# A spectral mixer with an MLP on one core: second batch's sums moved to GpSimd, its first stage ahead of the MLP, the last quarter of w_in converted between transform and MLP

## The chip, the core and the metric

The kernel runs on one NeuronCore of a Trainium2 chip. Its engines work side by side, each in the order of its own queue: PE (TensorE: matmuls, weight loads shown as PEld), DVE (VectorE), ACT (ScalarE, which also issues DMAs), POOL (GpSimd) and SP (SyncE, which here only issues DMAs). The metric is the time of one execution on the device in microseconds (us); lower is better.

## The reference, cut to what matters

```python
X = np.fft.rfft(x, axis=1)                    # x: 8 batches, 3008 positions, 256 columns
Yr = Xr @ w_r - Xi @ w_i + b_r
Yi = Xr @ w_i + Xi @ w_r + b_i
Y  = soft_threshold(Yr, 0.01) + 1j * soft_threshold(Yi, 0.01)
y  = np.fft.irfft(Y, n=3008, axis=1)
h  = y.reshape(24064, 256) @ w_in             # 256 x 2048
out = np.maximum(0.01 * h, h) @ w_out         # 2048 x 256
```

The MLP's two weights arrive as float64, and are turned into float32 (or a high and a low float32 part) on the chip.

## The kernel before, in words

The 3008-point transform is split as 47 x 64. For one batch the forward side is: `fwd`, the first stage over the 47, on seven tiles `xin` of 512 columns (the last has 256), which needs the sum and the difference of each tile's two halves and writes its results to `u_dram`; then `mid`, which for each of 12 pairs of rows reads `u`, does the second stage (`stage_b`: tile `ef`), multiplies by the spectral weights (`proj`: `kc`, then the threshold `t`, then `zf`), and turns back (`stage_g`: `v`, written to `v_dram`). The inverse's last stage (`inverse`: tiles `vin`, `odd`, `y`) makes the MLP's input `yc`, of which `forms` makes seven forms, each as a high and a low part (`yh`, `yl`), because the first MLP product is done with seven block products in place of eight. The MLP runs over 47 chunks of 512 tokens, in 8 steps each. One step (`moe_a`, `moe_b`, `moe_o`) has 21 matmuls with w_in, 12 with w_out, and on DVE five operations that end in `gl`.

Batches 0 and 1 are loaded ahead. Batch 0 goes through `fwd` and `mid` alone, before any MLP work; the later batches' forward sides are woven into the MLP as fill. The stretch between the last pair of batch 0's `mid` and the first MLP steps is called the turn here. In it also run the inverse of the first chunk and `fwd` of batch 1 (`stage_a1`), which before the change has no sums: for each of its two results it multiplies both halves of a tile, with the constants `fa0`, `fa1`, and a negated copy of `fa1` for the difference (`fa{h}` and `fa{2h}`), and so takes four products a tile. Five of its seven tiles are written ahead of the MLP in program order (`fp.to(0.69)`), two in the MLP's first steps.

The weights' conversions stand beside this: `convert_win` turns one of four quarters of w_in (`win_raw` into `win_hi`, `win_lo`, through the tiles `cva`, `cvq`, `ws`), the first two ahead of `mid` of batch 0, the others at its sixteenths 3 and 8, and `load_wout` turns one of eight pieces of w_out at each `next(wout)` (seven DVE operations and three of ACT), two in the turn and then one in each MLP step.

A scheduler reorders each engine's queue by its own estimates, within what `tc.issue_after` allows; so the order on an engine isn't the order of the code. Tiles with the same tag share buffers: a new tile waits until the old one's last reader is through. `forms` of the first chunk writes a `yh` buffer that held `ws`, and of the second one that held an `xin` of batch 1.

Of the kernel before, what the change touches and what calls it, by code (L numbers as in the profile page):

```python
# [8 lines left out]
F32 = mybir.dt.float32  # L9
# [11 lines left out]
P = 128  # L21
PA = NK1 * NG
# [8 lines left out]
def spectral_mlp_kernel(  # L31
# [18 lines left out]
    D = w_r.shape[0]  # L50
    DF = w_in.shape[1]
    NF = DF // P
    NH = D // P
# [10 lines left out]
    sb = ctx.enter_context(tc.tile_pool(name="sb", bufs=2))  # L64
# [4 lines left out]
    def bank(tag, bufs):  # L69
        return ps.tile([P, 512], F32, name=tag, tag=tag, bufs=bufs)  # L70

    def products(dst, pairs):

        terms = []
        for l, r in pairs:
            terms += [(l[0], r[0]), (l[0], r[1]), (l[1], r[0])] if len(l) == 2 else [(l[0], r[0])]
        for i, (a, b) in enumerate(terms):
            last = nc.tensor.matmul(dst, a, b, start=(i == 0), stop=(i == len(terms) - 1))  # L78
        return last
# [46 lines left out]
    def float64_parts(raw, a, q):  # L126


        wl, wh = raw[:, :, 0], raw[:, :, 1]
        u = a.bitcast(U32)  # L130
        act.mul(q, wl, 2.0 ** -52)
        act.activation(a, wh.bitcast(F32), AF.Abs, scale=2.0 ** 16)
        dve.tensor_scalar(a, a, F64_MIN * 2.0 ** 16, F64_MAX * 2.0 ** 16, ALU.max, ALU.min)
        dve.tensor_scalar(u, u, 4, 1, ALU.logical_shift_left, ALU.logical_shift_right)
        dve.scalar_tensor_tensor(u, wh, 0x80000000, u, ALU.bitwise_and, ALU.bitwise_or)
        dve.tensor_scalar(wl, u, 0xFF800000, None, ALU.bitwise_and)
        dve.tensor_mul(q, q, wl.bitcast(F32))
# [19 lines left out]
    def convert_win(c):  # L157


        a, q, s = win_tmp  # L160
        float64_parts(win_raw[c], a, q)
        dve.tensor_add(a, a, q)
        a = a.rearrange("p (j q i m) -> p j q i m", j=NH, q=2, i=2)
        a11, a12, a21, a22 = (a[:, j, :, i] for i in range(2) for j in range(2))
        dve.tensor_add(s[:, 0], a21, a22)
        dve.tensor_sub(s[:, 2], a11, a21)
        dve.tensor_sub(s[:, 1], s[:, 0], a11)
        dve.tensor_sub(s[:, 3], a12, s[:, 1])
        hi, lo = (w[:, :, 2 * c:2 * c + 2] for w in consts["win"])
        for k, w in ((slice(0, 2), a[:, :, :, 0]), (2, a22), (slice(3, 7), s)):  # L170
            act.copy(hi[:, k], w)
            last = dve.tensor_sub(lo[:, k], w, hi[:, k].bitcast(F32))
        return last
# [42 lines left out]
    def fwd(b):  # L216
        ud = dram.tile([2, NK1, NG * NS, D], F32, name="u_dram", tag="u_dram", bufs=NPRE + 1)
        u_dram[b] = ud
        uv = ud.rearrange("c k (g s) d -> c (k g) (s d)", g=NG)
        x_t, s_t = {}, {}  # L220

        def load(c):
            cols = slice(2 * c * D, min(2 * c + 2, NS) * D)
            n = cols.stop - cols.start
            if b < NPRE:
                tag, bufs = (XT, XT1)[b][c]
                x2 = sb.tile([PA, 2, 2 * D], F32, name="xin", tag=tag, bufs=bufs)
                x_t[c] = [x2[:, h, :n] for h in range(2)]
            else:
                x_t[c] = [  # L230
                    sb.tile([PA, 2 * D], F32, name=f"xin{h}", tag="uv"[h], bufs=3 - h)[:, :n] for h in range(2)
                ]
            for h, t in enumerate(x_t[c]):
                if b == 0:
                    (act if h else sync).dma_start(t, x[b, h, :, cols])
                else:
                    with tc.issue_after(reads[-1].ins):
                        sync.dma_start(t, x[b, h, :, cols])

        def fold(c):  # L240
            xa, xb = x_t[c]
            n = xa.shape[1]
            eng = pool if b else dve
            xs = sb.tile([PA, 2 * D], F32, name="xs", tag="e", bufs=1)[:, :n] if b else xs3[:, c % 3, :n]
            eng.tensor_add(xs, xa, xb)
            eng.tensor_sub(xa, xa, xb)
            s_t[c] = [(xs,), (xa,)] if b < NPRE else [xs, xa]

        def split(c, h):
            t = s_t[c][h]  # L250
            n = t.shape[1]
            z = sb.tile([PA, 2, 2 * D], F32R, name="xz", tag="z", bufs=1)
            xh, xl = z[:, 0, :n], z[:, 1, :n]
            dve.tensor_copy(xh, t)
            dve.tensor_sub(xl, t, xh.bitcast(F32))
            s_t[c][h] = (xh, xl)

        def stage_a(c, h):
            t = x_t[c][h]
            n = t.shape[1]  # L260
            pa = (bank("psf", 2) if b else bank("psh", 4))[:PA, :n]
            products(pa, [(consts[f"fa{h}"] if b else consts[f"fa{h}32"], s_t[c][h])])
            t = x_t[c][1 - h]
            cp = act.copy(t, pa)
            if b == 0:
                turned[:] = [cp]
            st = (act if b else sync).dma_start(uv[h, :, 2 * c * D:2 * c * D + n], t)
            if b == 0:
                written.append(st)

        def stage_a1(c):

            n = x_t[c][0].shape[1]
            pas = [(bank("psf", 2) if c in (4, 5) else bank("psh", 4))[:PA, :n] for _ in range(2)]
            for h in range(2):
                with tc.issue_after(turning[NPAIR - 2].ins):
                    products(pas[h], [
                        (consts[f"fa{h}32"], (x_t[c][0],)), (consts[f"fa{2 * h}32"], (x_t[c][1],))])
            for h in range(2):
                act.copy(x_t[c][h], pas[h])  # L280
                sync.dma_start(uv[h, :, 2 * c * D:2 * c * D + n], x_t[c][h])

        if b == 1:
            for c in range(NX):
                load(c)
                yield 0
            for c in (0, 1, 2, 3, 6, 4, 5):
                stage_a1(c)
                yield 6 * x_t[c][0].shape[1]
            return  # L290

        ahead = 2 if b >= NPRE else NX
        for c in range(ahead):
            load(c)
        yield 4 * CS if b >= NPRE else 0
        fold(0)
        if b >= NPRE:
            split(0, 0)
        yield 0
        for c in range(NX):  # L300
            for h in range(2):
                if h == 0 and c + ahead < NX:
                    load(c + ahead)
                if h == 0 and c + 1 < NX:
                    fold(c + 1)
                stage_a(c, h)
                if b >= NPRE and (c + h < NX):
                    split(c + h, 1 - h)
                yield 3 * x_t[c][h].shape[1]
# [335 lines left out]
    FWD = NS * 6 * D  # L645


    fa32 = sb.tile([PA, 3, PA], F32, name="fa32", tag="xi", bufs=1)
    for h in range(2):
        sync.dma_start(fa32[:, h], fa[h])  # L650
    for h in range(3):
        consts[f"fa{h}32"] = (fa32[:, h],)
    xs3 = sb.tile([PA, 3, 2 * D], F32, name="xs3", tag="yl")
    f0 = Stream(fwd(0), FWD)
# [22 lines left out]
    act.copy(bz[:1], brow[:1])  # L677
    act.copy(bz[32:33], brow[32:33])
    dve.tensor_sub(bz[32:33], brow[32:33], bz[32:33].bitcast(F32))
    act.mul(fa32[:, 2], fa32[:, 1], -1.0)  # L680
    convert_win(0)
    with tc.issue_after(turned[0].ins):
        split_consts()
# [12 lines left out]
    wout = load_wout()  # L696
    for i in range(1, 17):
        m0.to(i / 16)
        if i in (3, 8):
            convert_win(2 + i // 8)  # L700
        if 5 <= i < 12:
            next(fp.gen)
        if i == 13:
            next(wout)
    m0.finish()
    fp.to(0.69)
    for p in due[0]:
        v_load(p)
    for eh in range(NH):
# [1 line left out]
            inverse(p, eh)  # L711
    for _ in forms(0):
        pass
    next(wout)
    next(wout)


# [2 lines left out]
    for i, pos in enumerate(moe()):  # L720
        if i % 2 == 0 and len(converted) < NQ:
            with tc.issue_after(made[0].ins):
                next(wout, None)
        if i in (2, 4):
            with tc.issue_after(parted[0].ins), tc.issue_after(parted[1].ins):
                next(fp.gen)
        while cur + 1 < NB - 1 and pos >= (read[cur + 1] if cur >= 0 else 0):
            for s in streams:
                s.finish()
            cur += 1  # L730
            streams = ([Stream(fwd(cur + 1), FWD + 4 * CS)] if cur else []) + [mids[cur]]
        frac = (pos - read[cur]) / (read[cur + 1] - read[cur]) if cur + 1 < NB else 1
        if cur == 0:
            frac = max(0, frac - 0.2) * 1.25
        work = frac / 0.95 * sum(s.total for s in streams)
        with tc.issue_after(converted[-1].ins) if cur == 0 else nullcontext():
            for s in streams:
                s.to(work / s.total)
                work = max(0, work - s.total)
# [103 lines left out]
```

## Time and profile before

| | |
|---|---|
| median of 3 runs | 2600.41 us (2598.28 to 2602.9) |
| profiled execution | 2600.34 us, span 2598.6 us |
| mean granted PE clock | 0.993 |
| busy share of the span | PE 98%, DVE 73%, ACT 64%, POOL 9% |
| DMA, mean | 64 GB/s |

All times in the rows are counted from the start of the span. A row of the timeline has its start, its length, engine, line, operation, the tile written and the tiles read, and in brackets the idle time before it and what ended that. A matmul in float32 shows as two rows or passes in the trace (x4 is two such matmuls), and one instruction in the orders below. The lengths of matmuls overlap: what one takes of PE is read from start to start.

### The profile page before, as it was taken

What the parts mean: (1) busy time and instruction counts of PE and PEld (TensorE: products, weight loads), DVE (VectorE), ACT (ScalarE), POOL (GpSimd) and SP (SyncE); (2) the same over time, 40 slices, a digit from 0 to 9 for tenths busy, and PEclk for the clock granted to TensorE, in tenths of its full rate; (3) what the DMA queues carried; (4) which work ended last, traced back from release to release, by engine and by line L of the source; (5) the groups of instructions that cost most, each with busy time, mean ns of one, the idle gap of its engine ahead of it and who ended that gap; (6) DMA issues with size and microseconds to landing.
All of it is one profiled execution on the core that took longest, in us unless ns stands there. A gap on an engine that the chain in (4) does not pass through costs nothing.

```text
span 2598.6 us, 42643 instructions
## 1 busy us (share of the span) xinstructions
PE 2537.5 (98%) x16300; PEld 2281.5 (88%) x16300; DVE 1897.1 (73%) x3403; ACT 1668.5 (64%) x3174; POOL 229.6 (9%) x180
## 2 busy tenths in 40 slices
PE   5999999999999999999999999999999999999999
PEld 4689888999889998899988999889998889999998
DVE  7687786776777778777786777877777777767675
ACT  5766665776556666567665666566666667655564
POOL 0001121100110001100021000210002000000000
PEclk8999999999999999999999999999999999999999
DMA  8621132111221113211132111321113221101000
GB/s 259 179 85 50 48 89 72 54 47 48 82 78 49 45 41 90 75 55 51 33 97 68 49 49 37 104 67 49 49 36 101 64 58 48 44 17 32 9 17 17
DMA packets 119912, 165.13 MB, mean 64 GB/s; under 512 B 13601, under 2 KB 69917, under 8 KB 119709
## 3 DMA queue, kind: packets, MB, share of 16 engines
q1 hardware_dynamic: 79120, 115.55, 14.6%
q10 hardware_dynamic: 40589, 46.87, 7.1%
q8 instruction: 128, 2.10, 0.4%
q14 instruction: 75, 0.61, 0.1%
HBM read 86.60 MB, written 75.76 MB: 62 GB/s over the span
## 4 chain that ended last, share of the span: by engine, by line
PE 89%; DVE 3%; DMA 2%; ACT 1%; issue 0%; ACTq 0%; SPq 0%; DVEq 0%
PE pso L576 38%; PE psh L92 34%; PE psf L78 11%; PE psf L480 3%; PE psf L343 3%; DMA u<-u_dram 1%; DMA u_dram<-xin 1%; DVE yl L506 0%; DVE gl L563 0%; DMA raw<-w_out_dram 0%; DVE gf L557 0%; ACT gh L561 0%; DVE yt L511 0%; ACT gf L559 0%; DVE yc L512 0%
## 5 line engine op out<-in xcount | busy, mean ns | idle before, releaser
L92 PE MATMUL psh<-yh,win_hi 128*128 128x256 f32 x2632 | 752.3, 286 | 13.8 <-DVE gf L546 10.6
L92 PE MATMUL psh<-yl,win_hi 128*128 128x256 f32 x2632 | 738.3, 280 | 0.6 <-DVE yl L506 0.5
L92 PE MATMUL psh<-yh,win_lo 128*128 128x256 f32 x2632 | 737.9, 280 | 0.0
L576 PE MATMUL pso<-gh,wout_hi 128*128 128x512 f32 x1504 | 593.9, 395 | 0.0
L576 PE MATMUL pso<-gl,wout_hi 128*128 128x512 f32 x1504 | 591.1, 393 | 0.5 <-DVE gl L563 0.5
L576 PE MATMUL pso<-gh,wout_lo 128*128 128x512 f32 x1504 | 590.4, 393 | 0.0
L563 DVE TENSOR_TENSOR gl<-gf,gh 128x1024 fp32r<-128x1024 f32 x376 | 471.8, 1255 | 92.7 <-ACT gh L561 90.6
L92 PEld LDWEIGHTS psh<-yh,win_hi 128*128 128x128 f32 x2632 | 497.0, 189 | 30.7 <-DVE gf L546 15.4
L92 PEld LDWEIGHTS psh<-yl,win_hi 128*128 128x128 f32 x2632 | 497.0, 189 | 12.5 <-DVE yl L506 1.0
L92 PEld LDWEIGHTS psh<-yh,win_lo 128*128 128x128 f32 x2632 | 496.6, 189 | 0.2
L557 DVE TENSOR_TENSOR gf<-psh,u 128x512 f32<-128x512 f32 x376 | 259.1, 689 | 256.3 <-PE psh L92 255.1
L561 ACT CAST gh<-gf 128x1024 fp32r<-128x1024 f32 x376 | 396.4, 1054 | 7.1
L559 ACT ACTIVATE gf<-gf 128x768 f32<-128x768 f32 x376 | 320.0, 851 | 49.5 <-DVE gf L557 47.7
L576 PEld LDWEIGHTS pso<-gl,wout_hi 128*128 128x128 f32 x1504 | 282.5, 188 | 62.9 <-DVE gl L563 1.0
L576 PEld LDWEIGHTS pso<-gh,wout_hi 128*128 128x128 f32 x1504 | 283.1, 188 | 46.9 <-ACT gh L561 0.4
L576 PEld LDWEIGHTS pso<-gh,wout_lo 128*128 128x128 f32 x1504 | 282.9, 188 | 44.9
L556 ACT ACTIVATE gf<-psh 128x256 f32<-128x256 f32 x376 | 145.5, 387 | 266.6 <-PE psh L92 246.9
L542 ACT COPY p<-psh 128x256 f32<-128x256 f32 x376 | 140.1, 373 | 220.2 <-PE psh L92 219.1
L379 POOL TENSOR_TENSOR kb<-bias,kc 128x512 f32<-128x512 f32 x84 | 119.0, 1417 | 1530.6 <-ACT kc L376 1409.6
L543 DVE TENSOR_TENSOR u<-psh,p 128x256 f32<-128x256 f32 x376 | 158.6, 422 | 105.8 <-ACT p L542 103.5
L545 DVE TENSOR_TENSOR gf<-psh,u 128x256 f32<-128x256 f32 x376 | 159.3, 424 | 29.7 <-PE psh L92 2.0
L546 DVE TENSOR_TENSOR gf<-psh,gf 128x256 f32<-128x256 f32 x376 | 159.1, 423 | 9.0
(134 smaller groups left out, 3253.2 us busy)
## 6 DMA issues: line engine op xcount, KB each, us to landing
u<-u_dram SPq DMA_DIRECT2D x192, 128.0 KB, 2.7
v_dram<-v ACTq DMA_DIRECT2D x192, 128.0 KB, 2.4
out_dram<-ob SPq DMA_DIRECT2D x94, 256.0 KB, 2.1
vin<-v_dram SPq DMA_DIRECT2D x96, 240.0 KB, 3.5
xin<-x_dram SPq DMA_DIRECT2D x90, 240.0 KB, 3.0
u_dram<-xin ACTq DMA_DIRECT2D x72, 240.0 KB, 2.4
u_dram<-xin SPq DMA_DIRECT2D x24, 240.0 KB, 3.9
raw<-w_out_dram SPq DMA_DIRECT2D x8, 512.0 KB, 5.0
```

The costliest lines, as they stand in the source:

```text
L78: last = nc.tensor.matmul(dst, a, b, start=(i == 0), stop=(i == len(terms) - 1))
L92: mlp[:] = [nc.tensor.matmul(dst, a, b, start=start and i == 0, stop=i == 2, skip_group_check=True)]
L542: act.copy(p1, b1[:, lo])
L543: dve.tensor_add(u2, b1[:, hi], p1)
L545: dve.tensor_add(g[:, 3], b2[:, hi], u2)
L546: dve.tensor_add(g[:, 3], b2[:, lo], g[:, 3])
L556: act.activation(g[:, 0], b1[:, lo], AF.Prelu, alpha=SLOPE)
L557: dve.tensor_add(g[:, 1:3], b2.rearrange("p (k n) -> p k n", k=2), u2.unsqueeze(1).broadcast_to([P, 2, HT]))
L559: act.activation(g[:, 1:4], g[:, 1:4], AF.Prelu, alpha=SLOPE)
L561: cp = act.copy(gh, g)
L563: parted[:] = [cp, dve.tensor_sub(gl, g, gh.bitcast(F32))]
L576: mlp[:] = [nc.tensor.matmul(po, a[:, f, s], r[:, i], start=(f == 0 and j == 0), stop=(f == NF - 1 and j == 2),)]
```

## The change

Three things are done. GpSimd takes the sum and the difference of each of batch 1's seven tiles (`fold1`, 14 operations), writing the sum into the free half of the tile before it (a third slot in tile 4 serves the first); `stage_a1` then has two products a tile instead of four, the negated `fa1` goes, and the results of tiles 4 and 5 go to the `pso` banks instead of `psf`. All seven tiles of `stage_a1` stand ahead of the MLP (`fp.finish()`), none in its steps. The last quarter of w_in is converted behind `mid` instead of at its middle, in a tile of its own for `cva`; the third moves from sixteenth 3 to 4; and one piece of w_out instead of two is converted ahead of the MLP.

```diff
 def convert_win(c):
         a, q, s = win_tmp
+        if c == 3:
+            a = sb.tile([P, NH * NIN], F32, name="cva", tag="e", bufs=1)
...
 def load(c):   # in fwd
-                x2 = sb.tile([PA, 2, 2 * D], F32, name="xin", tag=tag, bufs=bufs)
+                spare = b == 1 and c == 4
+                x2 = sb.tile([PA, 3 if spare else 2, 2 * D], F32, name="xin", tag=tag, bufs=bufs)
                 x_t[c] = [x2[:, h, :n] for h in range(2)]
+                if b == 1:
+                    s_t[c] = x2[:, 1]
+                if spare:
+                    s_t[-1] = x2[:, 2]
...
+        def fold1(c):
+            xa, xb = x_t[c]
+            n = xa.shape[1]
+            xs = s_t[-1][:, :n]
+            s_t[-1] = s_t.pop(c)
+            pool.tensor_add(xs, xa, xb)
+            pool.tensor_sub(xa, xa, xb)
+            x_t[c] = [xs, xa]
+
         def stage_a1(c):
-            pas = [(bank("psf", 2) if c in (4, 5) else bank("psh", 4))[:PA, :n] for _ in range(2)]
+            pas = [(bank("pso", 2) if c in (4, 5) else bank("psh", 4))[:PA, :n] for _ in range(2)]
             for h in range(2):
                 with tc.issue_after(turning[NPAIR - 2].ins):
-                    products(pas[h], [
-                        (consts[f"fa{h}32"], (x_t[c][0],)), (consts[f"fa{2 * h}32"], (x_t[c][1],))])
+                    products(pas[h], [(consts[f"fa{h}32"], (x_t[c][h],))])
...
             for c in range(NX):
                 load(c)
                 yield 0
+            for c in (0, 1, 2, 3, 6, 4, 5):
+                fold1(c)
...
-    act.mul(fa32[:, 2], fa32[:, 1], -1.0)
...
-        if i in (3, 8):
-            convert_win(2 + i // 8)
+        if i == 4:
+            convert_win(2)
...
     m0.finish()
-    fp.to(0.69)
+    convert_win(3)
+    fp.finish()
...
     next(wout)
-    next(wout)
...
-        if i in (2, 4):
-            with tc.issue_after(parted[0].ins), tc.issue_after(parted[1].ins):
-                next(fp.gen)
```

What the scheduler makes of it: every engine's order is the same again from some 650 rows of PE on, where both have done the same work. The lines after the change are numbered 14 to 18 higher behind the first edits (L78 and L132 stay). On ACT, the last `ef` copy of batch 0 (its two sums open the last projection), before:

```order
L418 COPY v<-psh 128x512
L347 COPY ef<-psh 128x2x256
L420 DMA v_dram<-v 64x2x256
L396 COPY zf<-t 64x256
L400 ACTIVATE zf<-t,sign 64x256
```

and now, with the four zf instructions of pair 9 and a pair of stores ahead of it:

```order
L436 COPY v<-psh 128x512
L438 DMA v_dram<-v 64x2x256 x2
L414 COPY zf<-t 64x256
L418 ACTIVATE zf<-t,sign 64x256
L414 COPY zf<-t 64x256
L418 ACTIVATE zf<-t,sign 64x256
L365 COPY ef<-psh 128x2x256
```

The `ef` copy has moved behind pair 9's zf. Still on ACT, from the last pair's `kc` to the end of the transform (the last zf copies are pair 11's, the third `v` its result), before:

```order
L376 COPY kc<-pso 128x256
L318 DMA v_dram<-zero 48x256
L418 COPY v<-psh 128x512
L420 DMA v_dram<-v 64x2x256 x2
L418 COPY v<-psh 128x512
L396 COPY zf<-t 64x256 x2
L420 DMA v_dram<-v 64x2x256 x2
L418 COPY v<-psh 128x512
L132 ACTIVATE cva<-raw 128x512
```

and now:

```order
L394 COPY kc<-pso 128x256
L132 ACTIVATE cva<-win_raw 128x1024
L438 DMA v_dram<-v 64x2x256 x2
L436 COPY v<-psh 128x512
L336 DMA v_dram<-zero 48x256
L296 COPY xin<-pso 120x512
L438 DMA v_dram<-v 64x2x256 x2
L414 COPY zf<-t 64x256 x2
L296 COPY xin<-pso 120x512 x2
L436 COPY v<-psh 128x512
```

An activation of the quarter of w_in and a copy of the first stage stand ahead of the last zf, two more copies ahead of the last `v`. On PE, the turn from the last three `zf` products on (`fa` is the first stage of batch 1, `ga` the inverse), before:

```order
L78 MATMUL psh<-zf,w_105 128x512 x3
L78 MATMUL psh<-xin,fa_66 120x512 x8
L480 MATMUL psf<-ga,vin 128x128 x2
L78 MATMUL psh<-xin,fa_66 120x512 x2
L480 MATMUL psf<-ga,vin 128x128 x2
```

and now, from pair 10's on:

```order
L78 MATMUL psh<-zf,w_105 128x512
L78 MATMUL pso<-xin,fa_66 120x512 x3
L78 MATMUL psh<-zf,w_105 128x512
L78 MATMUL psh<-xin,fa_66 120x512 x3
L78 MATMUL pso<-xin,fa_66 120x512
L78 MATMUL psh<-xin,fa_66 120x512 x4
L498 MATMUL psf<-ga,vin 128x128 x2
L78 MATMUL psh<-xin,fa_66 120x512
L78 MATMUL psh<-xin,fa_66 120x256 x2
L498 MATMUL psf<-ga,vin 128x128 x10
```

Three products of the first stage now stand ahead of the last pair's, eight between it and the inverse, and three of 14 among the inverse's, where before it was none, eight and twelve of 20 (with the fences' next rows). On DVE, the third MLP step's end (`gl`) in the new order, with one whole piece of w_out (`cva`, `raw`, `cvq`, `wout_lo`) between two `gl`:

```order
L133 TENSOR_SCALAR cva<-cva 128x512
L134 TENSOR_SCALAR cva<-cva 128x512
L135 SCALAR_TENSOR_TENSOR cva<-raw,cva 128x512
L575 TENSOR_TENSOR gf<-psh,u_1051 128x512
L136 TENSOR_SCALAR raw<-cva 128x512
L137 TENSOR_TENSOR cvq<-cvq,raw 128x512
L203 TENSOR_TENSOR cva<-cva,wout_hi 128x512
L561 TENSOR_TENSOR u_1129<-psh,p_1128 128x256
L204 TENSOR_TENSOR wout_lo<-cva,cvq 128x512
L563 TENSOR_TENSOR gf<-psh,u_1129 128x256
L581 TENSOR_TENSOR gl<-gf,gh 128x1024
```

Before, six such pieces stood among the MLP's steps; now there are seven, and the second chunk's forms come ahead of the first `gl` instead of between the second and the fourth. SP's queue has stores of batch 1's first stage among its first four `vin` loads (three ahead of the first, three ahead of the second and third, two ahead of the fourth), where before they stood behind all four.

More of the change, by code (lines that the diff above doesn't have):

```diff
@@ L645, in spectral_mlp_kernel @@
     FWD = NS * 6 * D
-    fa32 = sb.tile([PA, 3, PA], F32, name="fa32", tag="xi", bufs=1)
+    fa32 = sb.tile([PA, 2, PA], F32, name="fa32", tag="xi", bufs=1)
     for h in range(2):
         sync.dma_start(fa32[:, h], fa[h])
-    for h in range(3):
+    for h in range(2):
         consts[f"fa{h}32"] = (fa32[:, h],)
```

## The prediction

> **What bounds the kernel now.** I read the page first (busy shares, chain), then the stretches around the hand-over from the first batch's transform to the MLP.
>
> ```profile
> PE 2537.5 (98%) x16300; PEld 2281.5 (88%) x16300; DVE 1897.1 (73%) x3403; ACT 1668.5 (64%) x3174; POOL 229.6 (9%) x180
> ...
> PE 89%; DVE 3%; DMA 2%; ACT 1%; issue 0%; ACTq 0%; SPq 0%; DVEq 0%
> ...
> 60.00:80.00 20.00, 18.91 (x97) 14.98 (x97) 18.09 (x34) 18.33 (x38) 0.00 (x0) 1.00 0.82 247
> 80.00:100.00 20.00, 19.01 (x94) 14.85 (x93) 11.64 (x23) 17.57 (x38) 0.30 (x1) 1.00 0.36 94
> 100.00:120.00 20.00, 17.40 (x48) 8.02 (x47) 10.44 (x19) 9.61 (x18) 0.00 (x0) 0.91 0.67 191
> 120.00:140.00 20.00, 17.27 (x92) 13.01 (x91) 16.24 (x37) 14.30 (x33) 0.00 (x0) 0.95 0.51 150
> 140.00:160.00 20.00, 18.28 (x99) 14.59 (x98) 18.17 (x37) 13.21 (x26) 0.00 (x0) 0.96 0.49 147
> 160.00:180.00 20.00, 19.39 (x124) 17.40 (x124) 19.86 (x39) 13.61 (x24) 0.00 (x0) 1.00 0.17 47
> 180.00:200.00 20.00, 20.00 (x136) 18.42 (x135) 13.06 (x23) 13.22 (x25) 2.58 (x2) 1.00 0.17 54
> ```
>
> The columns of a stretch are its length, busy us of PE, PEld, DVE, ACT and POOL, the granted clock, the DMA share and GB/s. PE is the bound, full from 180 us on. The order of every engine is the same again some 70 us later, so the change is worth what it does to the moment at which PE is through with the same MLP work near 180 us. Two stages lie before that: the turn (about 97 to 130 us), where PE idles little because the second batch's first stage fills it, and the ramp (130 to 180 us), where DVE, at 18.17 and 19.86 of 20 us, sets the pace while it converts w_out beside the MLP.
>
> ```profile
> 94.69 1.03 PE L78 MATMUL psf<-w,ef 128*128 128x256 f32 x4
> 97.52 1.02 PE L78 MATMUL psh<-zf,w 128*128 128x512 f32 x2
> 99.53 1.13 PE L78 MATMUL psh<-zf,w 128*128 128x512 f32 x2 [0.99 <-ACT zf L400]
> 103.26 1.48 PE L78 MATMUL psh<-zf,w 128*128 128x512 f32 x2 [2.60 <-ACT zf L396]
> 113.23 1.88 PE L78 MATMUL psh<-xin,fa 120*120 120x512 f32 x4
> 114.95 0.61 PE L480 MATMUL psf<-ga,vin 120*128 120x128 f32 x4
> 172.58 0.39 PE L576 MATMUL pso<-gl,wout_hi 128*128 128x512 f32 x1
> 172.81 0.39 PE L576 MATMUL pso<-gh,wout_hi 128*128 128x512 f32 x1
> 179.08 0.28 PE L78 MATMUL psf<-wr_hi,eh 128*128 128x256 f32 x1
> ```
>
> Here the last pair's projection begins at 94.69, the last three turns zf (pairs 9, 10, 11) stand at 97.52, 99.53 and 103.26, the last two after waits on ACT. The row at 179.08, the second batch's first projection, is my common point: in both orders exactly 162 products of w_in and 72 of w_out stand ahead of it.
>
> **The change, part by part.**
>
> *Half of the first stage's products go.* Two products of 512 columns take 114.95 - 113.23 = 1.72 us, 0.86 each. Twelve of 512 and two of 256 columns (half, 0.43) fall away: 11.2 us of PE work. It is gained only where PE is the bound, and behind it stand the other engines' chains.
>
> *The sums on GpSimd.* Fourteen operations, from the nearest rows:
>
> ```profile
> L246 POOL TENSOR_TENSOR xin<-xin,xin 120x512 f32<-120x512 f32 x36 | 50.9, 1414 | 2.8
> ...
> 398.31 1.30 POOL L246 TENSOR_TENSOR xin<-xin,xin 120x512 f32<-120x512 f32 x1
> 398.51 2.18 DVE L563 TENSOR_TENSOR gl<-gf,gh 128x1024 fp32r<-128x1024 f32 x1 [0.33 <-ACT gh L561]
> ...
> 81.67 1.06 SPq L238 DMA_DIRECT2D xin<-x_dram  x2
> 107.90 1.68 SPq L459 DMA_DIRECT2D vin<-v_dram  x4
> ...
> vin<-v_dram SPq DMA_DIRECT2D x8, 240.0 KB, 4.0
> ```
>
> At most 14 x 1.41 = 19.8 us of POOL. The last x tile is issued by 82.73; with the landing of a like transfer (4.0) it is there near 87, and the six operations that remain end near 95. Their first reader on PE comes after pair 10's turn, near 102, so they hide with 7 us to spare; if that cover went, PE would wait in front of pair 11's turn, and the zero store of v in ACT's queue (its memset now follows the sums in POOL's queue) would wait too. What they may cost is DVE: the gl of 398.51 took 2.18 instead of 1.22 (the row at 137.14 below), and ended 1.08 after the POOL operation beside it. Bounds for the fourteen: 0, and 14 x 0.96 = 13.4 us of DVE time. DVE is busy 11.64 of 20 at 80 to 100 us and loses the quarter's conversion before that, so I take 0.5 us on the path.
>
> *The order at the end of the transform.* The converted quarter, a piece of w_out and the first stage now stand among the last pairs' work.
>
> ```profile
> 92.47 0.59 ACT L347 COPY ef<-psh 128x512 f32<-128x512 f32 x1
> 93.23 0.41 ACT L396 COPY zf<-t 64x256 f32<-64x256 f32 x1 [0.16 <-ACT ef L347]
> 101.77 0.59 ACT L418 COPY v<-psh 128x512 f32<-128x512 f32 x1 [1.41 <-issue]
> 101.83 0.71 DVE L398 TENSOR_SCALAR zf<-t,sign 64x256 f32<-64x256 f32 x2
> 120.22 0.37 ACT L483 COPY odd<-psf 128x240 f32<-128x240 f32 x1
> 129.89 0.42 DVE L133 TENSOR_SCALAR cva<-cva 128x512 f32<-128x512 f32 x1
> ...
> L132 ACT ACTIVATE cva<-win_raw 128x1024 f32<-128x1024 f32 x4 | 4.5, 1134 | 0.0
> L280 ACT COPY xin<-psh 120x512 f32<-120x512 f32 (+1 forms) x10 | 5.3, 540 | 1.8 <-PE psh L78 1.8
> L171 ACT CAST win_hi<-ws 128x1024 fp32r<-128x1024 f32 x4 | 4.2, 1044 | 2.0 <-DVE ws L168 2.0
> ```
>
> The last ef copy moves behind pair 9's four zf instructions and two DMA issues (a copy of v waited 1.41 us for two such issues): from 92.47 to about 96.2, so the last projection, which had 2.2 us to spare, starts near 96.9 instead of 94.69: +2.2. Ahead of pair 11's zf then stand a 1.13 us activation of w_in and a 0.54 us copy on ACT and two operations on DVE: about +1 more. Pair 11's turn comes near 106.5 instead of 103.26 (bounds: 103.3, if these waits lie in what it waited for anyway, 2.60 us; and 108). ACT goes on 1.1 us behind it with 10.2 us of work (the 0.59 us copy of v, eleven copies at 0.54, casts of w_in of 1.04 and twice half of that, and three operations on w_out, half as wide as the 1.13 us one), waits some 1.4 us for products and DVE's parts, and comes to the first `odd` copy near 119.2; before, with PE's double products in the way, this was at 120.22. SP's four vin loads stand behind eight stores that wait for ACT, so the fourth is issued 8.5 us behind pair 11's turn instead of 6.3, and lands 4.0 later, near 119: as late as ACT. From the first `odd` to the end of the seven forms on DVE it took 129.89 - 120.22 = 9.7 us; PE, ACT and DVE have the same steps there, so it ends near 129.1 + 0.5 (POOL) = 129.6: -0.3.
>
> *The ramp.* One more eighth of w_out is converted there, and the tail of the first stage that filled PE is gone.
>
> ```profile
> 136.81 0.42 DVE L134 TENSOR_SCALAR cva<-cva 128x512 uint32<-128x512 uint32 x1
> 137.14 1.22 DVE L563 TENSOR_TENSOR gl<-gf,gh 128x1024 fp32r<-128x1024 f32 x1
> 138.28 0.69 DVE L135 SCALAR_TENSOR_TENSOR cva<-raw,cva 128x512 uint32<-128x512 uint32 x1
> 138.88 0.69 DVE L557 TENSOR_TENSOR gf<-psh,u 128x512 f32<-128x512 f32 x1
> ...
> 149.09 0.41 ACT L505 CAST yh<-yc 128x256 fp32r<-128x256 f32 x1 [2.32 <-DMA u_dram<-xin]
> ...
> 178.08 1.22 DVE L563 TENSOR_TENSOR gl<-gf,gh 128x1024 fp32r<-128x1024 f32 x1
> ```
>
> From start to start, DVE takes 0.33 (the small ones), 0.60 (512 wide) and 1.14 (gl). In the new order 84 operations stand between the end of the first forms and the gl of the sixth MLP step: six pieces of w_out (3.4 each, 20.5), the second chunk's forms (4.5) and the MLP's own (16.1), 41.1 us. The old order, summed likewise to the seventh gl, makes 45.2, and took 178.08 - 129.89 = 48.2: 3.0 us of waits, one of them behind the store that held a yh tile (149.09), which now leaves in the turn. I take 1.5 (bounds 0 and 3.0). The common point follows the sixth gl's 1.14 by ten output products (0.23 each) and three small ones (0.4): 41.1 + 1.5 + 1.1 + 2.3 + 0.4 = 46.4 us behind the forms, where before it was 179.08 - 129.89 = 49.2: -2.8.
>
> Sum: -0.3 - 2.8 = -3.1 us against the profiled execution's 2600.34 (span 2598.6, 1.7 around it): 2597.2, which is as much against the runs' median, 2600.41. Most of the 11.2 us becomes idle time of PE.
>
> The granted clock was 0.91 and 0.95 in the two stretches with gaps of PE, 1.00 beside them; more gaps may mean more of it, but the sum runs over DVE there. The Trainium skill, page "TensorE: Matmul & The Clock Gate", section "What's actually happening", has PE at half rate after an idle window of about 3.4 us. This trace shows the lower clock behind a gap of only 2.60 us. By the page's rule one such window more would cost 1.7 us of PE (an estimate), and the sum would be -1.4.
>
> **The rivals.**
>
> *PE stays the bound, faster.* If the last pair isn't late, the forms end 3.2 us earlier, and without waits in the ramp another 1.5: 2597.2 - 4.7 = 2592.5; with PE full throughout it would be 2600.34 - 11.2 = 2589.1. For it: ACT and DVE were at 18.33 and 18.09 of 20 at 60 to 80 us and now lose the quarter there. Against: PE still had 18.91 there, so little can be won.
>
> *POOL holds DVE, slower.* Up to about 95 us every sum can keep a two-input DVE operation waiting as at 398.51. If 10 of the 13.4 us fall on the thresholds that pair after pair feed ACT's zf, all that follows is late by as much: 2607. It decides from about 8 us on. Against: the quarter's DVE work leaves that very place. The Trainium skill, page "SBUF — State Buffer", section "Who interferes with whom", has the pair of ports as an exclusive lock for a whole instruction, two-input DVE operations included; the row at 398.51 agrees.
>
> *The ramp swallows it all.* With the old ramp's waits kept (3.0) and the last pair at 108, it is 2597.2 + 1.5 + 1.5 = 2600.2: no change, inside my forecast's own band.
>
> **How the numbers follow.** 0.2%, 5.2 us, is about what can be told from no change here. Forecast and swallowing ramp together 0.55 (own range 2593 to 2603), PE-bound 0.30, POOL lock 0.15. The forecast's low edge and the PE-bound case give faster 0.31, the lock and the late edge slower 0.14, same 0.55. The range runs from the floor 2589 to 2606.
>
> **What would show it.** Right: the POOL sums end before 97 us, pair 11's turn is near 106, PE idles 3 to 6 us before the MLP's steady start, DVE is full until the seventh gl, and the second batch's first projection stands near 176. Wrong: that projection near 170 (PE-bound), or the last projection of the first batch past 100 us with DVE waits beside POOL rows (lock).

## The result, and the profile after

The changed kernel takes 2623.96 us (median of 4 runs, 2622.76 to 2625.03) against 2601.65 for the kernel before (4 runs, 2598.28 to 2606.91): ratio 1.0084, 95% interval 1.0066 to 1.0102. It is slower by 22 us, outside the forecast range. The profiled execution took 2623.88 us.

From the page of the changed kernel, the busy shares and the chain:

```profile
PE 2547.5 (97%) x16272; PEld 2295.6 (88%) x16272; DVE 1904.5 (73%) x3403; ACT 1665.7 (64%) x3173; POOL 249.0 (9%) x194
...
PE 87%; DVE 4%; ACT 2%; DMA 1%; issue 1%; ACTq 0%; DVEq 0%
```

PE is still the bound, and it is busy 10.0 us longer than before (2537.5) with 11.2 us less to do. So PE not only waits more; it also works more slowly somewhere. The stretches of the hand-over, same columns as before:

```profile
60.00:80.00 20.00, 19.35 (x102) 15.41 (x101) 15.42 (x22) 15.93 (x33) 11.68 (x8) 1.00 0.88 260
80.00:100.00 20.00, 15.68 (x77) 11.68 (x75) 11.27 (x15) 13.77 (x30) 6.67 (x6) 1.00 0.30 70
100.00:120.00 20.00, 17.85 (x51) 8.79 (x52) 16.24 (x29) 16.11 (x31) 0.30 (x1) 1.00 0.56 146
120.00:140.00 20.00, 11.28 (x61) 9.82 (x60) 10.50 (x26) 10.38 (x27) 0.00 (x0) 0.83 0.71 245
140.00:160.00 20.00, 15.25 (x80) 13.84 (x81) 19.80 (x40) 13.16 (x22) 0.00 (x0) 0.74 0.09 28
160.00:180.00 20.00, 17.67 (x106) 15.33 (x105) 19.79 (x39) 13.50 (x22) 0.00 (x0) 1.00 0.29 91
180.00:200.00 20.00, 19.23 (x130) 17.50 (x129) 16.69 (x31) 11.54 (x22) 1.59 (x1) 1.00 0.15 41
...
50.00:220.00 170.00, 144.54 (x781) 117.82 (x780) 132.27 (x237) 113.69 (x225) 21.73 (x17) 0.95 0.42 124
```

The same long stretch of the kernel before:

```profile
50.00:220.00 170.00, 160.25 (x875) 128.40 (x875) 134.05 (x256) 120.48 (x241) 4.33 (x4) 0.98 0.45 129
```

The last two rows give a balance. PE idles 25.5 us instead of 9.8 (+15.7). The lower clock (0.95 and 0.98 of 170 us; 17.0 and 6.8 us at half rate) costs 5.1 us of work more. Less the 11.2 us of products that went, PE should be 9.6 us late near 200 us. The copies of the MLP's output (`ob`) show how late it is. Before:

```profile
191.85 1.06 ACT L581 COPY ob<-pso 128x512 f32<-128x512 f32 x2
...
747.85 0.59 ACT L581 COPY ob<-pso 128x512 f32<-128x512 f32 x1 [0.50 <-PE pso L576]
...
2594.81 0.59 ACT L581 COPY ob<-pso 128x512 f32<-128x512 f32 x1 [0.80 <-PE pso L576]
```

After:

```profile
200.74 0.59 ACT L599 COPY ob<-pso 128x512 f32<-128x512 f32 x1
...
757.02 0.59 ACT L599 COPY ob<-pso 128x512 f32<-128x512 f32 x1 [0.48 <-PE pso L594]
...
2618.37 0.58 ACT L599 COPY ob<-pso 128x512 f32<-128x512 f32 x1 [0.78 <-PE pso L594]
```

The first copy is 8.9 us late, the 22nd 9.2, and the last 23.6. There are two losses: about 9 us up to the MLP's steady start, and 14 us more that build up in small steps behind the 22nd copy, in the long stretch whose order is the same in both kernels. No new wait stands there. The groups of w_in's products between 850 and 2580 us (busy, mean ns of one | idle before) show where it is. Before:

```profile
L92 PE MATMUL psh<-yl,win_hi 128*128 128x256 f32 x1890 | 528.6, 280 | 0.5 <-DVE yl L506 0.5
L92 PE MATMUL psh<-yh,win_lo 128*128 128x256 f32 x1890 | 528.4, 280 | 0.0
```

After:

```profile
L92 PE MATMUL psh<-yh,win_lo 128*128 128x256 f32 x1872 | 529.6, 283 | 0.0
L92 PE MATMUL psh<-yl,win_hi 128*128 128x256 f32 x1873 | 528.6, 282 | 0.1
```

A w_in product takes about 2 ns more. From one start to the next (those of 400 ns and more, which hold a wait or another kind of product, left out) the means go from 117.2 to 120.6 ns (yh, win_lo), 117.3 to 119.1 (yl, win_hi) and 122.4 to 124.1 (yh, win_hi). There are 7896 of them (47 chunks x 8 steps x 21), so the average of 2.3 ns is 18 us in all, and 14 us for the 36 chunks behind the 22nd copy.

The instruction is the same. What differs is where its operands lie. With the negated `fa1`, `fa32` lost its third part (1440 to 960 bytes; the lines of the change ahead of the prediction don't show the tile, the first experiment's do), so its buffer, shared with `xi` (1024), shrank by 416 bytes, and every tile allocated behind it moved down: `yh` and `yl` begin 64 bytes past a multiple of 128 before, 32 past after. The weights `win_hi`, `win_lo` lie ahead of it and stay at 32 past.

### The profile page after: what moved, and what is told of

It reads as the page before. It is cut to its first block, busy times and chain, and to the rows that moved or that the text cites. A ratio compares the mean times of both kernels' runs of the same rounds, so it can differ in the third digit from the quotient of the medians.

```text
span 2622.1 us, 42609 instructions
## 1 busy us (share of the span) xinstructions
PE 2547.5 (97%) x16272; PEld 2295.6 (88%) x16272; DVE 1904.5 (73%) x3403; ACT 1665.7 (64%) x3173; POOL 249.0 (9%) x194
## 4 chain that ended last, share of the span: by engine, by line
PE 87%; DVE 4%; ACT 2%; DMA 1%; issue 1%; ACTq 0%; DVEq 0%
PE pso L594 37%; PE psh L92 34%; PE psf L78 11%; PE psf L498 3%; PE psf L361 3%; DVE gl L581 1%; DMA u<-u_dram 1%; DMA u_dram<-xin 1%; DVE yl L524 0%; DVE gf L575 0%; ACT gh L579 0%; ACT gf L577 0%; DVE yc L530 0%; ACT yh L523 0%; DVE yt L529 0%
## 5 line engine op out<-in xcount | busy, mean ns | idle before, releaser
L92 PE MATMUL psh<-yh,win_lo 128*128 128x256 f32 x2632 | 747.1, 284 | 0.0
```

What stands on the lines that cost most here:

```text
L92: mlp[:] = [nc.tensor.matmul(dst, a, b, start=start and i == 0, stop=i == 2, skip_group_check=True)]
```

## The experiments

Each was timed against the kernel before on the same chip; the ratios below are to it (2602 to 2603 us), with 95% intervals. The intervals are 5 to 7 us wide, so a difference of 3 to 5 us between two experiments is near the limit of what can be told.

**e1, only the place undone.**

```diff
-fa32 = sb.tile([PA, 2, PA], F32, name="fa32", tag="xi", bufs=1)
+fa32 = sb.tile([PA, 3, PA], F32, name="fa32", tag="xi", bufs=1)
```

> The changed kernel with one line back: the tile of the first-stage matrices keeps its third, now unused, part, so that every tile behind it in SBUF lies where it lay before the change (416 bytes higher); the order of all engines stays that of the changed kernel. Theory 'place': the 7896 products of w_in take some 2 ns longer each in the changed kernel (medians 119 to 120 ns from start to start against 117) because yh, yl and the other tiles no longer begin at a multiple of 64 bytes; then these products go back to 117 ns and 13 to 18 us come back: 2606 to 2611. Rival 'order': the loss lies in the order of the turn and the ramp alone, and the longer products are a matter of the run: 2624, products at 119 to 120 ns.

2610.34 us, ratio 1.0030 (1.0019 to 1.0041): 13.6 us come back. The w_in products are at 117.4 and 117.2 ns again, and the delay no longer grows: it is +10.4 at the common point (189.46 against 179.08), between 8.3 and 12.1 at the copies, and +10.4 at the last one (2605.22 against 2594.81). So 'place' holds, and 8 us are left for the turn and the ramp.

**e2, e3, e5: the kernel before, moved.** Its `fa32` tile is padded by 32 bytes (e2), by 96 (e5), or by 32 with the constant `sign` padded by 48, which moves the weights (e3); the order of every engine stays that of before.

```diff
-fa32 = sb.tile([PA, 3, PA], F32, name="fa32", tag="xi", bufs=1)
+fa32 = sb.tile([PA, 3 * PA + 8], F32, name="fa32", tag="xi", bufs=1)[:, :3 * PA]...   # e2; + 24 in e5
...
-sign = const.tile([P, NK1 + NPAIR], F32, name="sign")                                # e3, with e2's line
+sign = const.tile([P, 48], F32, name="sign")[:, :NK1 + NPAIR]
```

> The kernel before with the same tile 32 bytes longer, nothing else: all tiles behind it begin 32 bytes past a multiple of 64, the order is that of before. 'Place': the w_in products go from 117 to 119 or 120 ns, and the time from 2601.7 to 2615 to 2620. 'Order': 2601.7, no change.

> The kernel before with two paddings: the converted weights of w_in, which begin 32 bytes past a multiple of 64 in both kernels, are brought to a multiple of 64 as well, with yh and yl kept on one. If the place of the stationary operand counts as the moving one's does, the products get shorter by another 2 ns: 2584 to 2588. If only the moving operand's place counts, or 'order' holds: 2601.7.

> The kernel before with the tile of the first-stage matrices 96 bytes longer: yh, yl and all tiles behind it begin 32 bytes past a multiple of 128, as in the changed kernel (before: 64 past; 96 past and 0 past gave 2596.4 and 2597.1 with this order). Theory 'residue': 32 past a multiple of 128 is the bad place: the w_in products take 119 to 120 ns and the time is 2614 to 2618. Rival 'distance': what counts is how far the tiles lie from one another or from the weights (the changed kernel's lie 416 bytes lower, these 96 higher): products at 117 ns, 2596 to 2602.

e2: 2596.36, ratio 0.9978 (0.9969 to 0.9987). e3: 2597.13, 0.9979 (0.9970 to 0.9988). e5: 2615.59, 1.0049 (1.0037 to 1.0062). So the loss can be made in the kernel before by padding alone (e5, as 'residue' had it). But my first theory, that multiples of 64 are what is good, fell with e2: 32 bytes off such a multiple it is faster than before. e3's products (117.0 and 117.4 ns) got no shorter than e2's, and its time is neither of the two that were expected. The group of one product in e2 and e5, same window:

```profile
L92 PE MATMUL psh<-yh,win_lo 128*128 128x256 f32 x1897 | 530.1, 279 | 0.0
```

```profile
L92 PE MATMUL psh<-yh,win_lo 128*128 128x256 f32 x1876 | 530.8, 283 | 0.0
```

**e13, e14: which property of the place.** The weights are moved to 64 past a multiple of 128, with yh and yl at 64 past (e13) or 32 past (e14), by the same two paddings.

> The kernel before with two paddings: the weights of w_in begin 64 bytes past a multiple of 128 (32 before) and yh, yl and all behind them 64 past, as before. So far the bad place was 32 past, with the weights at 32 past too. Theory 'residue': only 32 past is bad for yh and yl, whatever the weights have: 2596 to 2603, w_in products at 117 ns. Rival 'equal': a product is slow where weights and moving operand have the same residue: 2614 to 2618, products at 119 to 120 ns.

> The same, with yh, yl and all behind them 32 bytes past a multiple of 128. 'Residue': 2614 to 2618, as with the weights at 32 past. 'Equal': 2596 to 2603.

e13: 2618.66, ratio 1.0059 (1.0046 to 1.0072): slow at the residue that was good before, as 'equal' had it and 'residue' not. e14: 2621.89, 1.0073 (1.0059 to 1.0087): slow again, which 'equal' did not have. The groups, e13 and then e14:

```profile
L92 PE MATMUL psh<-yh,win_lo 128*128 128x256 f32 x1877 | 531.2, 283 | 0.0
```

```profile
L92 PE MATMUL psh<-yh,win_lo 128*128 128x256 f32 x1871 | 527.5, 282 | 0.0
```

Both rivals fell in their first form; what all the runs have in common is the distance from the weights to the moving tiles, taken mod 128. The two mean columns are ns from one start to the next (850 to 2580 us, as above); the stretch is from the 22nd output copy to the last. In after, e2, e3 and e14 it holds one spell of 3.4 us at a granted clock of 0.50, which costs 1.7 us.

| kernel | win, mod 128 | yh and yl, mod 128 | distance, mod 128 | yh, win_lo | yl, win_hi | stretch, us |
|---|---|---|---|---|---|---|
| before | 32 | 64 | 32 | 117.2 | 117.3 | 1847.0 |
| e1 | 32 | 64 | 32 | 117.4 | 117.2 | 1848.2 |
| after | 32 | 32 | 0 | 120.6 | 119.1 | 1861.3 |
| e5 | 32 | 32 | 0 | 120.5 | 119.1 | 1857.7 |
| e13 | 64 | 64 | 0 | 120.5 | 119.2 | 1857.5 |
| e2 | 32 | 96 | 64 | 117.1 | 117.4 | 1842.0 |
| e3 | 64 | 0 | 64 | 117.0 | 117.4 | 1842.5 |
| e14 | 64 | 32 | 96 | 119.7 | 119.9 | 1862.1 |

Kernels with one distance agree to 0.2 ns. For 0 and 64 this holds with the weights at 32 and at 64; 32 and 96 were each made with one place of the weights only. Why the distance matters isn't shown: weight loads are busy 88% of the span beside products at 97%, so the two overlap, and a clash of their reads would fit, but no run separates it from others.

**The other 8 us.** Two of the reasons can be read in the changed kernel's trace. GpSimd and VectorE, near the end of the sums:

```profile
85.72 1.28 POOL L285 TENSOR_TENSOR xin<-xin 120x512 f32<-120x512 f32 x1
87.08 1.33 POOL L284 TENSOR_TENSOR xin<-xin 120x512 f32<-120x512 f32 x1
88.49 1.33 POOL L285 TENSOR_TENSOR xin<-xin 120x512 f32<-120x512 f32 x1
...
85.80 1.49 DVE L409 TENSOR_SCALAR c<-t 128x512 f32<-128x512 f32 x1
87.21 1.49 DVE L366 TENSOR_TENSOR ef<-ef 128x256 f32<-128x256 f32 x1
88.62 1.75 DVE L410 TENSOR_TENSOR t<-t,c 128x512 f32<-128x512 f32 x1
91.47 0.69 DVE L410 TENSOR_TENSOR t<-t,c 128x512 f32<-128x512 f32 x1
...
90.40 0.40 ACT L414 COPY zf<-t 64x256 f32<-64x256 f32 x1 [3.19 <-DVE t L410]
```

The first three VectorE operations each end 0.3 to 0.6 us behind the GpSimd operation beside them and take 1.5 to 1.75 us, where they take 0.4 to 0.7 alone; here the threshold's one-input `c` is held like the two-input ones. Fifteen VectorE operations overlap a GpSimd sum. Nine are longer than the shortest of their kind, by 7.8 us in all; six aren't, among them the four that read `psf` and `kc` (0.68 to 0.69 us). The three shown keep ACT's zf waiting 3.19 us. Further on:

```profile
101.01 1.03 PE L78 MATMUL psf<-w,ef 128*128 128x256 f32 x4
110.01 1.12 PE L78 MATMUL psh<-zf,w 128*128 128x512 f32 x2 [0.69 <-ACT zf L414]
133.26 3.75 PE L498 MATMUL psf<-ga,vin 120*128 120x128 f32 x16 [5.62 <-ACT yh L523]
187.59 0.39 PE L78 MATMUL psf<-wr_hi,eh 128*128 128x256 f32 x1 [0.77 <-ACT eh L376]
...
122.45 0.36 ACT L501 COPY odd<-psf 128x240 f32<-128x240 f32 x1 [1.15 <-PE psf L498]
128.92 0.66 ACT L131 ACTIVATE cvq<-raw 128x512 f32<-128x512 uint32 x1 [2.83 <-DMA raw<-w_out_dram]
...
135.45 0.42 DVE L133 TENSOR_SCALAR cva<-cva 128x512 f32<-128x512 f32 x1
179.70 1.22 DVE L581 TENSOR_TENSOR gl<-gf,gh 128x1024 fp32r<-128x1024 f32 x1
```

The last turn is at 110.01. ACT then stands 2.83 us, in its order, before a piece of w_out whose load SP issues only at 121.85, and PE idles 5.62 us behind it.

**e4, the sums on VectorE; e9, no sums at all** (both with e1's line). e9 leaves the sums out, so what it computes is no longer the reference's result; it serves for the time alone.

```diff
-            pool.tensor_add(xs, xa, xb)
-            pool.tensor_sub(xa, xa, xb)
+            dve.tensor_add(xs, xa, xb)        # e4; in e9 both are left out, and x_t[c] = [xa, xb]
+            dve.tensor_sub(xa, xa, xb)
```

> The changed kernel with the old place of the tiles (as in the first of these runs) and the fourteen sums of the second batch on VectorE instead of GpSimd. Theory 'lock': the waits of VectorE beside the last GpSimd sums (1.1 us each on three or four operations near 85 to 90 us) start the delay of the last pairs (last turn at 110.0 instead of 103.3); without GpSimd the last turn comes near 106 and the time is 3 to 6 us below that of the first run. Rival 'quarter': the converted quarter and the order around it delay the turn; then VectorE's additional 9 us make it no better: within 2 us of the first run, or slower.

> The changed kernel with the tiles at their old place (2610.3) and the fourteen sums left out altogether: the first stage of the second batch reads x as it comes, on no engine is anything added or subtracted. Theory 'lock': the sums on GpSimd lengthened nine VectorE operations by 7.8 us between 61 and 91 us, the last three of them on the thresholds of the last pairs; without them the time is at or below that of the sums on VectorE (2604.7): 2602 to 2605, and the last turn stands at 105 to 107. Rival 'order': the gain of the VectorE version came from its other order, not from the lock: 2608 to 2611, last turn at 109 or later.

e4: 2604.67, ratio 1.0012 (1.0003 to 1.0021), 5.7 us below e1. e9: 2606.51, 1.0017 (1.0008 to 1.0025), 3.8 below e1. The last turns of e1, e4 and e9:

```profile
112.47 1.13 PE L78 MATMUL psh<-zf,w 128*128 128x512 f32 x2 [0.77 <-ACT zf L414]
```

```profile
109.06 1.10 PE L78 MATMUL psh<-zf,w 128*128 128x512 f32 x2 [1.50 <-DVE zf L416]
```

```profile
106.40 1.13 PE L78 MATMUL psh<-zf,w 128*128 128x512 f32 x2 [0.76 <-ACT zf L412]
```

Without sums the turn is at 106.4, where 'lock' had it, and 6 us ahead of e1. But half of that lead is luck: these executions are apart before the first sum begins. A projection product of batch 0 that stands ahead of every sum (L78, `pso<-w,ef`) gives a start to count from:

| execution | sums on | that product, us | last turn, us | between, us |
|---|---|---|---|---|
| before | none | 57.30 | 103.26 | 45.96 |
| e2 (order of before) | none | 59.49 | 105.34 | 45.86 |
| e9 | none | 58.14 | 106.40 | 48.26 |
| e4 | VectorE | 60.70 | 109.06 | 48.36 |
| e11 (below) | VectorE | 58.74 | 109.41 | 50.67 |
| e1 | GpSimd | 61.44 | 112.47 | 51.03 |
| after | GpSimd | 57.89 | 110.01 | 52.12 |
| e15 (below) | GpSimd | 59.35 | 111.79 | 52.44 |

So the new order alone delays the last turn by 2.3 us (e9), and the sums on GpSimd by another 2.8 to 4.2. On VectorE they cost it 0.1 and 2.4 us. e4 has the time that 'lock' expected, but its turn is at 109.06 where 'lock' named 106. e9 has the turn, but its time lies midway between what 'lock' and 'order' expected. The intervals of both overlap with e1's, e4's just so; e15 against e11 below points the same way. So, taken together, 14 operations that VectorE does itself cost less than the same 14 on GpSimd. That e9 ends up 1.8 us behind e4 isn't settled: the ramps have other orders.

**e6, e7, e8: the quarter, the piece of w_out, both back** (with e1's line).

```diff
-        if c == 3:                          # e6, e8
-            a = sb.tile([P, NH * NIN], F32, name="cva", tag="e", bufs=1)
...
-        if i == 4:
-            convert_win(2)
+        if i in (3, 8):
+            convert_win(2 + i // 8)
...
-    convert_win(3)
...
     next(wout)                              # behind forms(0); e7, e8
+    next(wout)
```

> The changed kernel with the tiles at their old place (2610.3) and the last quarter of w_in converted where it was before, inside the transform; the sums stay on GpSimd. Theory 'quarter': the conversion's 1024-wide operations and the order about it hold up the last pairs; the last turn comes back from about 110 to 105 us and the time to 2604 to 2607. Rival 'lock': the last turn stays near 109 since the sums hold VectorE, which now has more to do beside them: 2608 to 2614.

> The changed kernel with the tiles at their old place (2610.3) and two pieces of w_out converted ahead of the MLP again instead of one. If the ramp is VectorE's, one piece of 3.4 us less there: 2606 to 2608. Rival: the piece delays the first forms by as much, or the ramp is held by TensorE's clock (17 us at half rate in the changed kernel): 2609 to 2613.

> Both of these: the quarter inside the transform and two pieces of w_out ahead of the MLP; what is left of the change is the sums on GpSimd, half the products and the first stage in one stretch ahead of the MLP. If the two add: 2600 to 2604, no better than before though TensorE has 11.2 us less to do; if the loss is the early first stage's own (nothing left to fill the ramp): 2607 to 2611.

e6: 2612.48, ratio 1.0037 (1.0024 to 1.0049): no better, as 'lock' had it, though its last turn comes at 114.30, not near 109. With the quarter's operations in VectorE's queue beside the sums, about a dozen operations are lengthened by some 9 us (counted as above). So e6 doesn't show what the quarter costs where no sums stand beside it. e7: 2607.09, 1.0016 (1.0007 to 1.0025): 3.2 us below e1, the size of one piece, though the two intervals overlap. e8: 2616.03, 1.0049 (1.0035 to 1.0062): neither expectation; the two don't add. VectorE's operations are lengthened by some 11 us there, and the sums end at 102 us, not 90.

**e10, the tail of the first stage back in the MLP** (with e1's line; tiles 4 and 5 use `psf` again).

```diff
-    fp.finish()
+    fp.to(0.69)
...
+        if i in (2, 4):
+            with tc.issue_after(parted[0].ins), tc.issue_after(parted[1].ins):
+                next(fp.gen)
```

> The changed kernel with the tiles at their old place (2610.3) and the last two blocks of the second batch's first stage behind the MLP's third and fifth step, as before the change. Theory 'filler': TensorE idles 9 to 11 us from 130 to 160 us and runs up to 20 us at half rate there, because nothing is left to fill the ramp; 3.4 us of products there and less ahead of the forms give 2 to 5 us back: 2605 to 2608. Rival 'VectorE's ramp': VectorE is at 19.8 of 20 us from 140 to 180, so filling TensorE changes nothing but the 2 us ahead of the forms: 2608 to 2611.

2614.10, ratio 1.0044 (1.0031 to 1.0057): 3.8 us above e1, with overlapping intervals. 'Filler' falls; 'VectorE's ramp' had no change, so it is off as well. PE is fuller up to 160 us than in the changed kernel, but the second batch's `mid` comes later (its first projection at 197.65), and PE idles where the kernel before had 19.39 and 20.00:

```profile
160.00:180.00 20.00, 16.15 (x93) 14.25 (x92) 17.21 (x34) 11.23 (x19) 0.00 (x0) 0.91 0.18 52
180.00:200.00 20.00, 17.07 (x108) 15.04 (x109) 16.67 (x32) 11.93 (x23) 0.00 (x0) 1.00 0.25 80
```

**e11, e12, e15, e16: put together.** All have distance 64 (`fa32` with a buffer of 1088 bytes) and two pieces of w_out ahead of the MLP; e11 the sums on VectorE, e15 on GpSimd, e12 is e11 with e10's tail, e16 is e11 with three pieces.

> The changed kernel with the sums on VectorE, two pieces of w_out ahead of the MLP, and the tiles 96 bytes past a multiple of 128. If the three add (5.7, 3.2, and 5.5 for the place): 2596, as the kernel before has it at that place (2596.4). If the VectorE time of the sums and the piece get into each other's way in the turn: 2598 to 2602.

> The same with the last two blocks of the first stage behind the MLP's third and fifth step, too. If 'filler' holds, 2 to 5 us below the one before: 2591 to 2594, below the kernel before at its best place (2596.4). If VectorE holds the ramp: within 2 us of it.

> The changed kernel with two pieces of w_out ahead of the MLP and the tiles 96 bytes past a multiple of 128; the sums stay on GpSimd. Against the version with the sums on VectorE (2595.4) this is the lock by itself. If it costs what it cost alone (5.7 us): 2600 to 2602. If the gain of the VectorE version came from its order in the ramp: 2595 to 2597.

> The version with the sums on VectorE, the tiles 96 past and three pieces of w_out ahead of the MLP instead of two. If the ramp is VectorE's and the turn has VectorE time to spare (13.95 of 20 us busy from 120 to 140): up to 3 us below 2595.4. If the third piece waits for its load, which begins behind the second's: 2595 to 2600.

e11: 2595.43, ratio 0.9972 (0.9961 to 0.9982): the three gains add, and it is faster than the kernel before and the changed one. But the kernel before at the same distance (e2) has 0.9978 (0.9969 to 0.9987), so the change as mended can't be told from none. e15: 2599.95, 0.9988 (0.9979 to 0.9997): the sums on GpSimd cost 4.5 us more here than on VectorE (e11), 4.2 by the ratios. e12: 2599.15, 0.9988 (0.9979 to 0.9997): 3.7 us above e11, neither expectation; the tail gains nothing here either. e16: 2602.93, 0.9998 (0.9990 to 1.0007): the third piece costs 7.5 us, more than either expectation. Part of it is that ACT waits for its load ahead of the next forms (all waits for such loads from 110 to 150 us: 4.6 us, 1.4 in e11):

```profile
145.78 0.66 ACT L131 ACTIVATE cvq<-raw 128x512 f32<-128x512 uint32 x1 [2.84 <-DMA raw<-w_out_dram]
146.34 0.60 ACT L523 CAST yh<-yc 128x512 fp32r<-128x512 f32 x1
```

## Why the prediction was wrong, step by step

**The premise, the step that failed first.** "The order of every engine is the same again some 70 us later, so the change is worth what it does to the moment" near 180 us. With the tiles at their old place that is so (+10.4 at the common point and at the end, e1). But the same order isn't the same time: the distance of moving tiles from weights changed from 32 to 0 (mod 128), which is 13.6 of the 22.3 us. The smaller `fa32` was read as the loss of a constant, and no term of the sum, no rival and no bound had it.

**The sum up to the common point.** It had the common point at 176.0 us (129.6 + 46.4), and it came at 187.59. The 11.6 us between the two are 3.3 up to the first `odd`, 2.6 from there to the end of the forms, 1.7 in the ramp up to the sixth gl and 4.1 behind that. The paragraphs below take them in turn.

**The lock, a rival too small.** Of 0 to 13.4 us of VectorE time I took 0.5 on the path. The trace has 7.8 of VectorE time. The sums on GpSimd delay the last turn by 2.8 to 4.2 us, and the times of the runs put 4 to 6 on the path (3.8 in e9, 5.7 in e4, 4.5 in e15). The mechanism, and the sign that would show it (the last projection past 100 us: it is at 101.01), stood in the prediction; that VectorE is idle half of that stretch was taken for cover. It isn't, where an operation that is held is a link of the chain from pair to pair. The rule of the Trainium skill that the prediction weighed (page "SBUF — State Buffer", section "Who interferes with whom") gives the lock to two-input operations and to those in a two-port mode; the one-input `c` at 85.80 was held, too, which would fit the second; no run shows the mode.

**The order at the end of the transform.** Last projection: 96.9 forecast, 101.01 measured; last turn 106.5 (bounds to 108), 110.01; first `odd` 119.2, 122.45. The order itself was forecast well: without the sums (e9) the last projection is at 97.40, the last turn at 106.40 and the first `odd` at 120.15, though with a start 0.8 us later than in the profile before. What was missing is the sums' delay. With the quarter back in its old place (e6) nothing is won, but there it stands beside the sums.

**From the first odd to the forms' end.** I took 9.7 us, as before, and it is 13.0: 2.83 of the difference is ACT's wait for `raw`. The piece's load stands behind the first stage's stores in SP's queue; that queue was followed for `vin` and not for `raw`. So the forms end at 135.45, not 129.6. In e9, where the wait is 1.26 us, the stretch still takes 11.7.

**The ramp.** The sixth gl is 44.25 us behind that (179.70 - 135.45), where 41.1 + 1.5 was forecast: the counting of VectorE's operations was right to 1.7 us. The end of it was not: from the sixth gl to the common point it takes 7.9 us instead of 3.8, because PE was behind: when that gl ended it still had 23 w_in products to do ahead of the common point (14 in the kernel before). That its gaps and its time at half rate had put it behind is likely but not shown by itself; e9 takes 7.8 us there, so it isn't the lock's doing. That one piece of w_out is worth its 3.4 us of VectorE fits e7 (3.2).

**The 11.2 us.** Forecast: most of it becomes idle time of PE. It did, and more: 15.7 us more of idle time and 5.1 us lost by the clock stand against it. Not all of this is the change's: in five other profiles with the order of before, the product of the table above comes 2.2 to 3.9 us later than in the one that the forecast was built on, and the common point 2.5 to 6.6 us later (181.54 to 185.66).

## What to carry to other kernels

When an edit changes the size of any tile, compare where all tiles lie before and after, and time the old order at two or three paddings first: here 32 bytes were worth up to 25 us (e3 and e14), more than the edit itself. An elementwise operation that goes to GpSimd isn't free for VectorE: count what stands beside it, and if that is a chain with links shorter than the GpSimd operation, a link can be lengthened to it (here nine operations of fifteen were longer). A position in one execution can be off by some us from the start on, so count from a point ahead of the change. An equal order proves equal time only where the addresses are equal too.

## What the runs showed of the hardware that was not expected

The place: w_in products at 117 ns for distances of 32 and 64 bytes (mod 128) between weights and moving tile, at 119 to 120.6 ns for 0 and 96, eight kernels in all. The output products, whose two operands moved together, changed as well (gl with wout_hi: 231.0 ns before, 229.3 after, 228.7 in e2), and in e13 it is 229.2 ns with both operands at the residues of before, so the operands of neighbouring instructions matter, too. In the Trainium skill, page "SBUF — State Buffer", section "Who interferes with whom", the moving operand and the weights come through two independent read ports and PE never waits on anyone. Here a w_in product takes 1.7 to 3.4 ns more with nothing changed but addresses; whether that arises at the ports isn't shown.

The clock: in the changed kernel the matmuls go from 0.28 to 0.42 us at 142.68 and back only at 152.81.

```profile
141.34 0.38 PE L92 MATMUL psh<-yh,win_hi 128*128 128x256 f32 x1 [1.78 <-DVE gf L564]
142.39 0.28 PE L92 MATMUL psh<-yh,win_lo 128*128 128x256 f32 x1
142.68 0.42 PE L92 MATMUL psh<-yl,win_hi 128*128 128x256 f32 x1
152.81 0.28 PE L92 MATMUL psh<-yh,win_lo 128*128 128x256 f32 x1
```

The longest gap in the 3 us ahead of that is 1.78 us, and the granted clock from 142.5 to 152.8 us is 0.50. So a gap much shorter than the 2.60 us of the prediction's row was followed by 10 us at half rate, in which two more (1.42 and 1.99 us) fall. In the kernel before, gaps of 0.83 and 0.68 us are followed by 3.4 us at 0.50 from 138.0 on.
